# Transformer block on one core: output projection from packed heads, row sums kept in memory, three open VectorE units, layernorm pieces in the fast queue

## The chip, the cores and the metric

The kernel runs on one core of a Trainium2 chip. The time is the device time of one execution, in microseconds; the median of the runs counts. The engines that matter here are TensorE (PE, matrix products; its weight loads are PEld), VectorE (DVE), ScalarE (ACT, which makes the exponentials), GpSimd (POOL) and SyncE (SP), whose instruction queue issues every DMA of this kernel. Each engine works off its instructions strictly in order.

## What is computed

A transformer block over 2048 rows of width 640, with 32 heads of 20 columns, in bf16:

```python
x = A_x
h  = x + attention(layernorm(x)) @ wo        # qkv = layernorm(x) @ wqkv; softmax(q k^T / sqrt(20)) v, 32 heads
h2 = h + ((layernorm(h) @ w_gate) * (layernorm(h) @ w_up)) @ w_down   # 640 -> 1728 -> 640
```

The softmax needs 32 x 2048 x 2048 exponentials, and that is what the kernel is built around.

## The kernel before

**Layout.** Heads are held in 8 groups of 4. A group fills 128 partitions: each head has a slot of 32, of which 20 hold values and one holds the head's sum of exponentials; the rest is padding. `qa`/`qb` and `kT` are queries and keys per group, `vx` the values with a column of ones. `On[g]` is the normalised attention output of group g for the current block of 512 query rows, still in slots of 32, and `wo[g]` the 80 rows of the output weight that belong to it, spread over the same slots with zeros between.

**Tiles.** Scores are made in tiles `sc` of 128 partitions x 1536 columns of PSUM, two buffers, 683 tiles in all. A segment is one group in one pass: pass "0" is query block 0, passes "1", "2", "3" are whole later blocks, and "E"/"F", "C"/"D", "A"/"B" are the halves of blocks 1, 2 and 3. For each tile PE makes the scores (`emit_S`, L557), ACT takes the exponential of the tile (L573, into `E` or `El`), and PE multiplies the result with `vx` into `acc` (`emit_AV`, L795).

**VectorE's units.** Where the planner finds VectorE free, the last 512 of the 1536 columns go to it instead (`x_takes`, `emit_x`): four operations, first `xv` from the scores (L610), two on `xt` (L620, L621) and last `xe` (L615). ACT's instruction then has 1024 columns. A unit is open from its first operation to its last; at most two may be open (`len(x_open) < 2`), and `xv` and `xt` have two buffers each.

**The planner.** The order of all instructions is written out when the program is built. For each tile a planner adds up estimated costs for PE, ACT and VectorE (the dictionary `at`) and fills the time that PE has over with pieces of other work: projections, the output projection `out`, the gated layer `glu`, and `y`. For VectorE, `spare` puts pieces between: first those of the queue `hot`, then units if their segment ends soon, then the queue `aux`, then units. Where PE would run too little full-width work it inserts products whose result is not used (`keep_warm`, L508, and in `emit_S`, L553).

**Normalising a group.** When a segment is done, `acc` is copied to `asb` (L807). `norm` stores the four rows of sums to a small memory tensor (L666), loads them back spread over partitions into a column range of `sums_all` (L667), takes reciprocals (L677), stores and broadcasts them (L679, L682), and multiplies into `On[g]` (L685). Each is a DMA in SP's queue. The last group of a half (`FAST`, and the last of all) does the same on PE instead (`sums_on_pe`, `rows_to_cols`), and copies its sums to `sums_all` (L711). At the end `flag_ok` checks the range of all 512 columns of `sums_all`.

**The second half of the block.** When the groups of half a block are normalised, `add_tail` queues `out`, `glu` and `y` for it. `out_mm` multiplies 8 groups into one bank of 320 columns (L1052), adds the input rows (L1056), and the second layernorm follows (`ln2_pieces`, queued on `aux`). The last half block has nothing to hide behind: `last_tail` runs after the last exponential, and there `out_most` makes 7 products per bank (L1378) before group 7 is normalised, and `out_last` the eighth (L1382).

Of the kernel before, what the change touches and what calls it, by code (L numbers as in the profile page):

```python
# [40 lines left out]
FPW = 256  # L41
G1 = 4
SPLIT_G = {"1": 4, "2": 2, "3": 1}
QA = 3 * QB
# [47 lines left out]
def kernel(  # L92
# [80 lines left out]
    def wqk_half(c, hf):  # L173
        return (wo if hf else wqk)[c][:, 0:D].rearrange("p (m x) -> p m x", m=2)

# [417 lines left out]
    def x_takes(i):  # L593
        us, n = tiles[i]
        s = us[-1][0]
        whole = segs[s][4] == "only"
        if not whole and (aux or last_tile[s] - i < X_CHUNK):
            return False
        return (n == EW and (PASS[segs[s][0]][0] < LAST_B or room()) and last_tile[s] - i >= X_LEAST and len({u[0] for u in us if not whole and u[3] >= n - BANK or whole}) == 1
                and len(x_open) < 2 and at["dve"] < at["pe"] + PE_DVE + TOL and len(x_live) < X_OUT)  # L600

    def emit_x(ps, us):
        s = us[0][0]
        w = PASS[segs[s][0]][2]
        v = xp.tile([P, BANK], F32, name="xv", bufs=2)
        u = v[:].bitcast(U16).rearrange("p (n h) -> p n h", h=2)[:, :, 0]
        t = xp.tile([P, BANK], F32, name="xt", bufs=2)
        e = xp.tile([P, BANK], I16, name="xe", bufs=X_OUT)
        dve(608, 0)
        took = nc.vector.tensor_scalar(v[:], ps, X_SCALE, X_BASE, ALU.mult, ALU.max)  # L610
        x_live.append((s, us[-1][1], us[-1][2]))
        x_left[s] = x_left.get(s, 0) + 1

        def last():
            nc.vector.scalar_tensor_tensor(e[:], t[:], X_R, v[:], ALU.mult, ALU.add)  # L615
# [3 lines left out]
        x_open.append((s, deque([  # L619
            lambda: nc.vector.scalar_tensor_tensor(t[:], u, X_P, u, ALU.add, ALU.mult),  # L620
            lambda: nc.vector.scalar_tensor_tensor(t[:], t[:], X_Q, u, ALU.add, ALU.mult),  # L621
            last])))
        x_last[0] = x_open[-1]
        return took
# [31 lines left out]
    def read_out(b):  # L656
        return all(("om", b, t) in done for t in TAILS[b])

    def norm(s, asb):
        p, g = segs[s][0:2]  # L660
        b, c0, w = PASS[p]
        n = w // 32
        r16 = sums_all[:, col["n"]:col["n"] + n]
        col["n"] += n
        sums = dram.tile([HPG, w], F32, name="sums", tag=f"sums{w}")
        nc.sync.dma_start(sums[:], asb[DH:P:SLOT, 0:w])  # L666
        nc.sync.dma_start(r16, sums[:].rearrange("j (c f) -> (j c) f", f=n))  # L667

        due = at["dve"] + SUMS_NS

        def back():
# [4 lines left out]
            dve(130)  # L676
            nc.vector.reciprocal(ri[:], r16)  # L677
            scr = dram.tile([HPG, w], F32, name="scr", tag=f"scr{w}")
# [5 lines left out]
            def times(asb, bc, p, g, c0, w):  # L684
                nc.vector.tensor_tensor(On[g][:, c0:c0 + w], asb[:, 0:w], bc[:, 0:w], ALU.mult)  # L685
# [16 lines left out]

    def sums_to_rows(ps, w):
        n = w // SLOT
        r16 = sums_all[:, col["n"]:col["n"] + n]
        col["n"] += n
# [3 lines left out]
        nc.vector.tensor_copy(bc[:, 0:w].rearrange("p (j e) -> p j e", e=SLOT), ri[:].rearrange("p (j e) -> p j e", e=1).to_broadcast([P, n, SLOT]))  # L710
        nc.vector.tensor_copy(r16, ps[:, 0:n])  # L711
        return bc
# [6 lines left out]
    def job_norm(s, asb):  # L719
# [4 lines left out]
        dve(700, 0)  # L724
        bc = sums_to_rows(ps, w)
        yield NEXT
# [258 lines left out]
    def load_wo():  # L985
        for g in range(NG):
            nc.vector.memset(wo[g][:], 0.0)
# [5 lines left out]
            while at["pe"] < due and not now["forced"]:  # L993
                yield WAIT

    def make_identf():
# [50 lines left out]
    def out_mm(on, st, t):  # L1047
        for hf in range(2):
            ps = bank()
            cs = slice(hf * HALF, (hf + 1) * HALF)  # L1050
            for g in range(NG):
                nc.tensor.matmul(ps[:, 0:HALF], lhsT=on[g][:, t * P:(t + 1) * P], rhs=wo[g][:, cs],  # L1052
                                 start=(g == 0), stop=(g == NG - 1))
                if g == NG - 1:
                    dve(408, 136)
# [80 lines left out]
    def job_out(on, st, ts, key):  # L1136
# [229 lines left out]
    def last_tail():  # L1366
# [6 lines left out]
        def out_most(t, hf):  # L1373
            ps = ps_h[t, hf] = bank()
            cs = slice(hf * HALF, (hf + 1) * HALF)
            nc.tensor.matmul(ps[:, 0:HALF], lhsT=ident[:], rhs=st["xr"][t][:, cs], start=True, stop=False)
            for g in range(NG - 1):
                nc.tensor.matmul(ps[:, 0:HALF], lhsT=on[g][:, t * P:(t + 1) * P], rhs=wo[g][:, cs], start=False, stop=False)  # L1378

        def out_last(t):  # L1380
            for hf in range(2):
                nc.tensor.matmul(ps_h[t, hf][:, 0:HALF], lhsT=on[NG - 1][:, t * P:(t + 1) * P],  # L1382
                                 rhs=wo[NG - 1][:, hf * HALF:(hf + 1) * HALF], start=False, stop=True)
# [47 lines left out]
    def fill():  # L1431
        while step() is not None:
            pass

    def flag_ok():
        n = col["n"]
        bits = sums_all[:, 0:n].bitcast(I32)
        nc.vector.tensor_reduce(ext[:, 0:1], bits, axis=AX.X, op=ALU.min)
# [76 lines left out]
    def general():  # L1515
        st = new_st(None)
        st["res"] = {}
        with tc.For_i(0, S, P) as r0:
# [3 lines left out]
            for g in range(NG):  # L1522
# [41 lines left out]
                nc.tensor.transpose(ps[:], oq[:].rearrange("p j e -> p (j e)"), ident[:])  # L1564
                nc.vector.tensor_copy(On[g][:, 0:P], ps[:])
            for fn in (job_out(On, st, [0], None), job_glu(st, [0]), job_y(st, [0])):
# [35 lines left out]
```

## Time and profile before

| | us |
|---|---|
| median of 3 runs | 896.84 (896.48 to 897.79) |
| the profiled execution, device time | 900.67 |
| its span, first to last instruction | 898.8 |
| first exponential starts | 16.22 |
| last exponential ends (857.62 + 1.14) | 858.76 |

The profiled execution is 3.83 us above the median of the runs. The span has three parts: 16 us before the first exponential, 842.5 us in which ACT works off the 683 tiles, and 40 us after them. In the views, "idle before" is the time an engine stood still just ahead of an instruction, and the name behind the arrow is what released it. "PEclk" is the clock that TensorE was granted, as a share of full speed.

### The profile page before, as it was taken

How to read it: one execution, taken by the hardware profiler on the slowest of the kernel's cores; microseconds unless marked ns; L12 is line 12 of the kernel's file. 1: busy time of each engine (PE TensorE's matmuls, PEld its weight loads, DVE VectorE, ACT ScalarE, POOL GpSimd, SP SyncE). 2: the span in 40 equal slices, each digit the busy share in tenths (PEclk: the TensorE clock that was granted, in tenths of full speed). 3: DMA queues.
4: the chain of work that ended last, by engine and by line, in shares of the span. 5: the costliest groups of instructions: out<-in, count | busy, mean ns of one | idle time of the engine just before them, and what ended most of it. 6: DMA issues, size and time to landing. Idle time of an engine off the chain costs nothing.

```text
span 898.8 us, 21965 instructions
## 1 busy us (share of the span) xinstructions
PE 813.7 (91%) x8921; PEld 374.1 (42%) x8921; DVE 773.7 (86%) x1448; ACT 852.7 (95%) x719; POOL 31.4 (3%) x122
## 2 busy tenths in 40 slices
PE   7889999989999899889999998998899999999997
PEld 5333232222233344544444554443434455444465
DVE  7778899999999899789999998999889988889842
ACT  6999999999999999989999999999999999999951
POOL 4100000000002000001000000001000000000000
PEclk9999999999999999989999999999989999999999
DMA  6030010011034556432214334111441312010310
GB/s 198 25 65 2 1 28 25 15 36 28 14 84 112 122 146 198 112 88 66 54 51 122 81 96 107 47 30 29 121 121 45 85 31 74 15 44 9 94 38 18
DMA packets 110763, 60.15 MB, mean 67 GB/s; under 512 B 37976, under 2 KB 107652, under 8 KB 110656
## 3 DMA queue, kind: packets, MB, share of 16 engines
q1 hardware_dynamic: 110656, 58.68, 25.0%
q8 instruction: 72, 1.18, 0.6%
q14 instruction: 35, 0.29, 0.1%
HBM read 48.09 MB, written 7.28 MB: 62 GB/s over the span
## 4 chain that ended last, share of the span: by engine, by line
ACT 56%; PE 21%; issue 13%; DVE 9%; DMA 1%; SPq 0%; ACTq 0%; DVEq 0%
ACT E L573 46%; ACT El L573 10%; PE sc L557 5%; PE mi L1221 3%; PE acc L795 3%; PE f L1203 2%; PE mi L306 1%; PE mi L1052 1%; DVE xv L610 1%; PE mi L1270 1%; PE f L1270 1%; DVE xt L620 1%; DVE xt L621 1%; DVE xe L615 1%; DVE hh L1229 1%
## 5 line engine op out<-in xcount | busy, mean ns | idle before, releaser
L573 ACT ACTIVATE E<-sc 128x1536 bf16<-128x1536 f32 (+1 forms) x560 | 694.0, 1387 | 7.3 <-PE sc L557 6.0
L557 PE MATMUL sc<-qa,kT 32*128 32x256 bf16 (+1 forms) x2176 | 204.1, 320 | 23.8 <-ACT E L573 13.5
L557 PEld LDWEIGHTS <-kT 32*128 32x128 bf16 x3136 | 85.2, 92 | 223.9 <-issue 193.4
L610 DVE TENSOR_SCALAR xv<-sc 128x512 f32<-128x512 f32 x199 | 137.1, 690 | 47.3 <-PE sc L557 44.4
L573 ACT ACTIVATE El<-sc 128x1536 bf16<-128x1536 f32 (+1 forms) x123 | 159.7, 1371 | 0.6 <-PE sc L557 0.5
L795 PE MATMUL acc<-E,vx 128*32 128x256 bf16 (+1 forms) x2245 | 158.2, 315 | 0.6 <-DVE vx L271 0.6
L615 DVE SCALAR_TENSOR_TENSOR xe<-xt,xv 128x512 int16<-128x512 f32 x199 | 134.3, 681 | 0.8
L621 DVE SCALAR_TENSOR_TENSOR xt<-xt,xv 128x512 f32<-128x512 f32 x199 | 133.2, 680 | 0.6
L620 DVE SCALAR_TENSOR_TENSOR xt<-xv 128x512 f32<-128x512 uint16 x199 | 132.1, 679 | 0.3 <-DVE ri L677 0.2
L306 PE MATMUL mi<-lnT,wp 128*128 128x512 bf16 x305 | 86.5, 381 | 7.1 <-DVE qa L313 3.4
L795 PEld LDWEIGHTS <-vx 128*32 128x32 bf16 x3136 | 62.2, 96 | 62.5 <-issue 60.6
L557 PE MATMUL sc<-qb,kT 32*128 32x256 bf16 (+1 forms) x960 | 69.0, 283 | 3.4 <-ACT E L573 2.2
L1270 PE MATMUL mi<-wd,hh 128*128 128x320 bf16 x378 | 65.5, 301 | 1.1 <-DVE xr L1274 1.0
L1221 PE MATMUL mi<-ln2T,wg 128*128 128x256 bf16 x390 | 56.7, 274 | 8.6 <-DVE u L1226 7.2
L1221 PE MATMUL mi<-ln2T,wu 128*128 128x256 bf16 x390 | 55.5, 274 | 7.4 <-DVE hh L1229 7.2
L795 PE MATMUL acc<-El,vx 128*32 128x256 bf16 (+1 forms) x579 | 60.6, 294 | 0.5 <-ACT El L573 0.5
L795 PE MATMUL acc<-xe,vx 128*32 128x256 bf16 (+1 forms) x312 | 57.3, 306 | 0.0
L1270 PEld LDWEIGHTS <-hh 128*128 128x128 bf16 x448 | 37.9, 97 | 29.5 <-issue 18.2
L1221 PEld LDWEIGHTS <-wg 128*128 128x128 bf16 x390 | 33.6, 97 | 30.0 <-issue 25.3
L306 PEld LDWEIGHTS <-wp 128*128 128x128 bf16 x310 | 24.8, 97 | 50.6 <-issue 38.5
L1221 PEld LDWEIGHTS <-wu 128*128 128x128 bf16 x390 | 33.8, 97 | 28.3 <-issue 25.1
L1052 PE MATMUL mi<-wo,on 128*128 128x320 bf16 x224 | 41.6, 312 | 2.3 <-DVE xr L1056 2.2
(152 smaller groups left out, 623.0 us busy)
## 6 DMA issues: line engine op xcount, KB each, us to landing
wu<-in_B_w_up_dram SPq DMA_DIRECT2D x38, 320.0 KB
wg<-in_B_w_gate_dram SPq DMA_DIRECT2D x37, 320.0 KB
bc<-scr SPq DMA_DIRECT2D x60, 64.0 KB
bc<-scr SPq DMA_DIRECT2D x108, 32.0 KB
qsp<-qa SPq DMA_DIRECT2D x8, 384.0 KB
xr<-in_A_x_dram SPq DMA_DIRECT2D x16, 160.0 KB
out_dram<-xr SPq DMA_DIRECT2D x14, 160.0 KB
wd<-in_B_w_down_dram SPq DMA_DIRECT2D x13, 160.0 KB
```

What stands on the lines that cost most here:

```text
L306: nc.tensor.matmul(ps[:], lhsT=wslice(m, g, c), rhs=lnT[:, c, ch * QB:(ch + 1) * QB], start=(c == 0), stop=(c == KT - 1))
L557: nc.tensor.matmul(sc[:, o:o + w], lhsT=kT[g][SLOT * j:SLOT * (j + 1), kt * P:(kt + 1) * P], rhs=q_of(g, b, c0, w)[SLOT * j:SLOT * (j + 1) ...
L573: exps = nc.scalar.activation(e[:, 0:n_act], sc[:, 0:n_act], ACT.Exp, bias=EXP_BIAS, scale=SM_SCALE)
L610: took = nc.vector.tensor_scalar(v[:], ps, X_SCALE, X_BASE, ALU.mult, ALU.max)
L615: nc.vector.scalar_tensor_tensor(e[:], t[:], X_R, v[:], ALU.mult, ALU.add)
L620: lambda: nc.vector.scalar_tensor_tensor(t[:], u, X_P, u, ALU.add, ALU.mult),
L621: lambda: nc.vector.scalar_tensor_tensor(t[:], t[:], X_Q, u, ALU.add, ALU.mult),
L795: nc.tensor.matmul(acc["t"][SLOT * j:SLOT * (j + 1), 0:w], lhsT=vx[kt][:, VS * h:VS * h + SLOT], rhs=e, start=(acc["n"][j] == 0), stop=(ac ...
L1052: nc.tensor.matmul(ps[:, 0:HALF], lhsT=on[g][:, t * P:(t + 1) * P], rhs=wo[g][:, cs], start=(g == 0), stop=(g == NG - 1))
L1203: nc.tensor.matmul(ps[:, 0:n], lhsT=st["w", fp][k][:, c, f_cols(fp, f2)], rhs=st["ln2T"][:, c, c0:c0 + n], start=(c == 0), stop=(c == KT - 1))
L1221: nc.tensor.matmul(ps[:, f2 * n:(f2 + 1) * n], lhsT=st["w", fp][k][:, c, f_cols(fp, f2)], rhs=st["ln2T"][:, c, c0:c0 + n], start=(c == 0), ...
L1270: nc.tensor.matmul(ps[:, 0:HALF], lhsT=st["hh"][f // 2][:, f % 2, t * P % HW:t * P % HW + P], rhs=late["Wd"][f][:, cs], start=(f == 0), st ...
```

## The change

1. **Packed projection.** Groups 0 to 5 no longer go to `wo` and `On` in slots of 32. Their 24 heads are 480 dense rows in four pairs of tiles, `d0` to `d3`, of 128, 128, 128 and 96 rows. The multiplication of a group writes a scratch tile `on` (two buffers), and `pack` copies its heads by DMAs in SP's queue, four, or five where a head crosses a tile's end. Groups 6 and 7 stay as they were. A bank takes 6 products for 8; `out_most` 5 for 7.
2. **Sums in memory.** `sums_all` is a memory tensor of 512 columns for 128 rows. `keep_sums` stores each segment's sums there, also those of the groups normalised on PE, whose copy on VectorE goes. `read_sums` loads all of them in `last_tail`, for `flag_ok`.
3. **A third open unit.** `x_open` may hold three; `xv` gets a third buffer; `xt` keeps two, taken at the unit's second operation.
4. **Queue.** `ln2_pieces` and the multiplication `times` go to `hot`. The planner's costs for `out` are lower.

```diff
+PADDED = (6, 7)
+DENSE = ("d0", "d1", "d2", "d3")
+OUT_ROWS = {"d3": 96}
+X_OPEN = 3
-PE_NS = {"out": 6000, "glu": 23000, "y": 7000}
+PE_NS = {"out": 4900, "glu": 23000, "y": 7000}
-ALONE_NS = {"out": 4350, "glu": 15260, "y": 5710}
+ALONE_NS = {"out": 3264, "glu": 15260, "y": 5710}
-    wo = [const.tile([P, D], BF16, name=f"wo{g}") for g in range(NG)]
+    wo = {k: const.tile([P, D], BF16, name=f"wo{k}") for k in DENSE + PADDED}
-    sums_all = const.tile([P, N_SUMS], F32, name="sums_all")
+    sums_all = dram.tile([P * N_SUMS], F32, name="sums", bufs=1)
-    On = [onp.tile([P, QB], BF16, name=f"on{g}") for g in range(NG)]
+    On = {k: onp.tile([P, QB], BF16, name=f"on{k}") for k in DENSE + PADDED}
...
-                and len(x_open) < 2 and at["dve"] < at["pe"] + PE_DVE + TOL and len(x_live) < X_OUT)
+                and len(x_open) < X_OPEN and at["dve"] < at["pe"] + PE_DVE + TOL and len(x_live) < X_OUT)
-        v = xp.tile([P, BANK], F32, name="xv", bufs=2)
+        v = xp.tile([P, BANK], F32, name="xv", bufs=X_OPEN)
...
+    def pack(o, g, cols):
+        for j in range(HPG):
+            r, d = DH * (HPG * g + j), 0
+            while d < DH:
+                n = min(DH - d, P - (r + d) % P)
+                to = (r + d) % P
+                nc.sync.dma_start(On[DENSE[(r + d) // P]][to:to + n, cols], o[SLOT * j + d:SLOT * j + d + n, cols])
+                d += n
+
+    def keep_sums(asb, w):
+        n = w // SLOT
+        sums = sums_all[P * col["n"]:P * (col["n"] + n)]
+        col["n"] += n
+        nc.sync.dma_start(sums.rearrange("(j q) -> j q", j=HPG), asb[DH:P:SLOT, 0:w])
+        return sums
...
-        sums = dram.tile([HPG, w], F32, name="sums", tag=f"sums{w}")
-        nc.sync.dma_start(sums[:], asb[DH:P:SLOT, 0:w])
-        nc.sync.dma_start(r16, sums[:].rearrange("j (c f) -> (j c) f", f=n))
+        sums = keep_sums(asb, w)
+        r16 = nrm.tile([P, n], F32, name="r16", tag=f"r{n}")
+        nc.sync.dma_start(r16[:], sums.rearrange("(q f) -> q f", f=n))
...
-                nc.vector.tensor_tensor(On[g][:, c0:c0 + w], asb[:, 0:w], bc[:, 0:w], ALU.mult)
+                cols = slice(c0, c0 + w)
+                o = On[g] if g in PADDED else onp.tile([P, QB], BF16, name="on", bufs=2)
+                nc.vector.tensor_tensor(o[:, cols], asb[:, 0:w], bc[:, 0:w], ALU.mult)
+                if g not in PADDED:
+                    pack(o, g, cols)
-                aux.append(times(asb, bc, p, g, c0, w))
+                hot.append(times(asb, bc, p, g, c0, w))
...
-        nc.vector.tensor_copy(r16, ps[:, 0:n])
...
+    def out_product(ps, key, t, cs, start, stop):
+        n = OUT_ROWS.get(key, P)
+        nc.tensor.matmul(ps[:, 0:HALF], lhsT=On[key][0:n, t * P:(t + 1) * P], rhs=wo[key][0:n, cs], start=start, stop=stop)
...
-            for g in range(NG):
-                nc.tensor.matmul(ps[:, 0:HALF], lhsT=on[g][:, t * P:(t + 1) * P], rhs=wo[g][:, cs],
-                                 start=(g == 0), stop=(g == NG - 1))
+            for key in DENSE + PADDED:
+                out_product(ps, key, t, cs, key == DENSE[0], key == PADDED[-1])
...
-            aux.append(ln2_pieces(st, pair, key))
+            (hot if key is not None else aux).append(ln2_pieces(st, pair, key))
...
-            for g in range(NG - 1):
-                nc.tensor.matmul(ps[:, 0:HALF], lhsT=on[g][:, t * P:(t + 1) * P], rhs=wo[g][:, cs], start=False, stop=False)
+            for key in (DENSE + PADDED)[:-1]:
+                out_product(ps, key, t, cs, False, False)
...
-        bc = sums_to_rows(sums_on_pe(asb, HW), HW)
+        bc = sums_to_rows(sums_on_pe(asb, HW), HW, asb)
+        read_sums()
...
+    def read_sums():
+        assert col["n"] == N_SUMS
+        final["sums"] = nrm.tile([P, N_SUMS], F32, name="bc")
+        nc.sync.dma_start(final["sums"][:], sums_all[:].rearrange("(q f) -> q f", f=N_SUMS))
```

Since the planner's rules change, the order moves on every engine. Counted over the whole order, VectorE has 208 units for 199, PE 192 products of the output projection for 256, and of the products that only keep it busy 118 at L508 for 112 and 17 at L553 for 18. The number of score tiles is the same.

VectorE while the keys and queries of later groups are still being projected (`kT`, `qa`; L618, L615, L629 and L623 are a unit's four operations in turn), in the changed kernel:

```order
L618 TENSOR_SCALAR xv<-sc 128x512 x3
L317 TENSOR_SCALAR kT_146<-mi,one_row 128x512
L836 TENSOR_TENSOR qa_121<-acc,qa_121 128x512
L615 SCALAR_TENSOR_TENSOR xt<-xv 128x512 x2
L317 TENSOR_SCALAR kT_146<-mi,one_row 128x512
L629 SCALAR_TENSOR_TENSOR xt<-xt,xv 128x512 x2
L623 SCALAR_TENSOR_TENSOR xe<-xt,xv 128x512
L317 TENSOR_SCALAR kT_146<-mi,one_row 128x512
L623 SCALAR_TENSOR_TENSOR xe<-xt,xv 128x512
L615 SCALAR_TENSOR_TENSOR xt<-xv 128x512
```

Three units are begun in a row here, and the third waits with its second operation until the two others are through; before, a third could not begin.

VectorE's last stretch ahead of the last score tile's value products; the last `asb` copy is that of the last segment. Before:

```order
L615 SCALAR_TENSOR_TENSOR xe<-xt,xv 128x512 x2
L708 RECIPROCAL ri<-mi 128x8
L710 COPY bc<-ri 128x256
L711 COPY sums_all<-mi 128x8
L685 TENSOR_TENSOR on_173<-asb,bc 128x256
L731 TENSOR_TENSOR on_174<-asb,mi 128x256
L807 COPY asb<-acc 128x256
```

and now:

```order
L733 RECIPROCAL ri<-mi 128x8
L735 COPY bc<-ri 128x256
L623 SCALAR_TENSOR_TENSOR xe<-xt,xv 128x512
L755 TENSOR_TENSOR on_170<-asb,mi 128x256
L709 TENSOR_TENSOR on<-asb,bc 128x256
L1304 TENSOR_TENSOR xr<-mi,xr 128x320
L831 COPY asb<-acc 128x256
```

Group 5's multiplication of the last half (L685, now L709) moved behind group 6's (L731, now L755), and the copy of sums is gone.

SP's queue at the same place, from the last normalisation by DMA to the weights of the last part. Before:

```order
L679 DMA scr<-ri 128x8
L682 DMA bc<-scr 32x256 x4
L1280 DMA out_dram<-xr 128x640 x2
L1169 DMA E<-in_B_w_up_dram 128x5x256
L1169 DMA E<-in_B_w_gate_dram 128x5x256
```

and now:

```order
L680 DMA sums<-asb 4x256
L1310 DMA out_dram<-xr 128x640
L673 DMA ond_169<-on 20x256 x4
L680 DMA sums<-asb 4x256
L1468 DMA bc<-sums 128x512
L1310 DMA out_dram<-xr 128x640
L1199 DMA E<-in_B_w_up_dram 128x5x256
L1199 DMA E<-in_B_w_gate_dram 128x5x256
```

Four copies of heads into `d3`, two stores of sums and the load of all sums stand in the queue where two stores of output rows stood.

More of the change, by code (lines that the diff above doesn't have):

```diff
@@ L604, in emit_x, with second @@
         w = PASS[segs[s][0]][2]
-        v = xp.tile([P, BANK], F32, name="xv", bufs=2)
+        v = xp.tile([P, BANK], F32, name="xv", bufs=X_OPEN)
         u = v[:].bitcast(U16).rearrange("p (n h) -> p n h", h=2)[:, :, 0]
-        t = xp.tile([P, BANK], F32, name="xt", bufs=2)
+        t = []
+        def second():
+            t.append(xp.tile([P, BANK], F32, name="xt", bufs=2))
+            nc.vector.scalar_tensor_tensor(t[0][:], u, X_P, u, ALU.add, ALU.mult)
         e = xp.tile([P, BANK], I16, name="xe", bufs=X_OUT)
@@ L619, in emit_x @@
         x_open.append((s, deque([
-            lambda: nc.vector.scalar_tensor_tensor(t[:], u, X_P, u, ALU.add, ALU.mult),
-            lambda: nc.vector.scalar_tensor_tensor(t[:], t[:], X_Q, u, ALU.add, ALU.mult),
+            second,
+            lambda: nc.vector.scalar_tensor_tensor(t[0][:], t[0][:], X_Q, u, ALU.add, ALU.mult),
             last])))
@@ L701, in sums_on_pe, with sums_to_rows @@
         return ps
-    def sums_to_rows(ps, w):
+    def sums_to_rows(ps, w, asb):
         n = w // SLOT
-        r16 = sums_all[:, col["n"]:col["n"] + n]
-        col["n"] += n
+        keep_sums(asb, w)
         ri = nrm.tile([P, n], F32, name="ri", tag=f"ri{n}")
@@ L724, in job_norm @@
         dve(700, 0)
-        bc = sums_to_rows(ps, w)
+        bc = sums_to_rows(ps, w, asb)
         yield NEXT
@@ L1564, in general @@
                 nc.tensor.transpose(ps[:], oq[:].rearrange("p j e -> p (j e)"), ident[:])
-                nc.vector.tensor_copy(On[g][:, 0:P], ps[:])
+                o_t = On[g] if g in PADDED else onp.tile([P, QB], BF16, name="on", bufs=2)
+                nc.vector.tensor_copy(o_t[:, 0:P], ps[:])
+                if g not in PADDED:
+                    pack(o_t, g, slice(0, P))
             for fn in (job_out(On, st, [0], None), job_glu(st, [0]), job_y(st, [0])):
```

21 lines of the change are left out of this document (10 added, 11 removed).

## The prediction, made before the changed kernel ran

> **What bounds the kernel now.** I read the page first: busy shares, the slices, the chain.
>
> ```profile
> PE 813.7 (91%) x8921; PEld 374.1 (42%) x8921; DVE 773.7 (86%) x1448; ACT 852.7 (95%) x719; POOL 31.4 (3%) x122
> ACT  6999999999999999989999999999999999999951
> PEclk9999999999999999989999999999989999999999
> ACT 56%; PE 21%; issue 13%; DVE 9%; DMA 1%; SPq 0%; ACTq 0%; DVEq 0%
> ```
>
> ACT is the busiest engine and is full in all slices but the first and the last two. That is an average, so next the windows, cut at the first and the last exponential, and ACT's waits.
>
> ```profile
> 16.20:858.80 842.60, 768.72 (x8520) 338.33 (x8521) 745.19 (x1362) 835.28 (x684) 24.57 (x61) 0.99 0.25 65
> 858.80:898.80 40.00, 33.46 (x277) 26.10 (x276) 16.06 (x48) 9.91 (x24) 0.00 (x0) 0.96 0.11 32
> ACT E L573 <- PE sc L557: 6.0, 8, 2.0
> ACT El L573 <- PE sc L557: 0.5, 2, 0.3
> ```
>
> In the 842.6 us of the loop (columns: length, then PE, PEld, DVE, ACT, POOL busy) ACT works 835.28 and waits for scores 6.5, in ten places. So in the loop time is what ACT is given to do, plus those few waits; an edit on PE or VectorE is worth nothing there by itself. In the 40 us after it ACT has 9.91 us of work and PE sets the pace. The change is to be priced in these two parts separately.
>
> **Term 1, exponentials moved to VectorE: -3.8 us.** The order has 208 units for 199, so nine more tiles go through ACT with 1024 columns instead of 1536.
>
> ```profile
> L573 ACT ACTIVATE E<-sc 128x1536 bf16<-128x1536 f32 x397 | 561.3, 1511 | 4.5 <-PE sc L557 3.4 <-PE acc L795 0.4 <-ACT El L573 0.3
> L573 ACT ACTIVATE E<-sc 128x1024 bf16<-128x1024 f32 x163 | 171.7, 1082 | 2.8 <-PE sc L557 2.6 <-ACT E L573 0.2
> L573 ACT ACTIVATE El<-sc 128x1536 bf16<-128x1536 f32 x86 | 124.9, 1498 | 0.3 <-PE sc L557 0.3
> L573 ACT ACTIVATE El<-sc 128x1024 bf16<-128x1024 f32 x37 | 39.7, 1075 | 0.3 <-PE sc L557 0.2
> ```
>
> A unit saves ACT 1511 - 1082 = 429 ns, or 1498 - 1075 = 423 in the other buffer: 9 x 0.427 = 3.8 us. The third open unit therefore buys only nine, although 484 tiles went without a unit before. The reason is VectorE:
>
> ```profile
> L610 DVE TENSOR_SCALAR xv<-sc 128x512 f32<-128x512 f32 x199 | 137.1, 690 | 47.3 <-PE sc L557 44.4
> 837.23 0.69 DVE L610 TENSOR_SCALAR xv<-sc 128x512 f32<-128x512 f32 x1
> 837.84 0.41 DVE L807 COPY asb<-acc 128x256 f32<-128x256 f32 x1
> ```
>
> One operation lasts 0.69 us and the next starts 0.61 after it, so a unit is four times 0.61, 2.4 us of VectorE, and nine are 22. VectorE stands idle 842.6 - 745.2 = 97 us in the loop, 47 of them ahead of a unit's first operation, while it waits for scores. The nine fit into that, so I cost them at nothing. If they did not, see rival B.
>
> **Term 2, the tail: -1.0 us.** The chain after the last exponential:
>
> ```profile
> 859.20 0.24 PE f L1376
> 859.45 0.95 PE f L1378 x7
> 860.40 0.34 PE f L700 x4
> 860.74 0.16 PE f L1376
> 860.89 0.95 PE f L1378 x7
> 861.84 0.44 PE acc L716 x4
> 862.29 0.14 PE f L1376
> 862.42 0.95 PE f L1378 x7
> 863.37 0.27 PE f L1382 x2
> 863.65 0.14 PE f L1376
> 863.78 0.95 PE f L1378 x7
> ```
>
> Seven products take 0.95 us, 0.136 each. Each of the four banks loses two, so PE is through 8 x 0.136 = 1.09 us earlier. VectorE must keep up:
>
> ```profile
> 859.24 0.42 DVE L807 COPY asb<-acc 128x256 f32<-128x256 f32 x1 [5.98 <-PE acc L795]
> 861.07 0.29 DVE L710 COPY bc<-ri 128x256 f32<-128x256 f32 x1
> 864.91 0.89 DVE L209 BATCH_NORM_STATS2 st<-f 128x6 f32<-128x320 f32 x2 [0.22 <-PE f L1382]
> ```
>
> The sums on PE (L700) started at 860.40 and can now start 0.27 earlier, at 860.13; `asb` is there at 859.66. `bc` ends at 861.36, moves with them to 861.09, and PE asks for it at 860.74 - 0.27 + 0.16 + 0.68 = 861.31. Before the statistics of the second row tile VectorE had waited 0.22 us. The first row tile comes six products, 0.82 us, earlier, the second eight, 1.09: of the 0.27 between them 0.22 are covered and 0.05 lost. 1.0 us remains; the bounds are 1.1 and, if VectorE were late everywhere, 0.
>
> **Term 3, products taken from the loop: 0, between -4.5 and +4.6.** The loop's 28 banks lose 56 products of 0.136, 7.6 us of PE. PE is not what ACT waits for, except here:
>
> ```profile
> 285.00:295.00 10.00, 7.96 (x55) 1.64 (x53) 8.95 (x22) 9.40 (x8) 4.58 (x7) 0.83 0.52 103
> 397.00:406.00 9.00, 9.00 (x98) 4.12 (x95) 6.05 (x13) 6.68 (x6) 0.00 (x0) 0.62 0.01 2
> 651.00:664.00 13.00, 12.12 (x78) 4.26 (x79) 9.85 (x21) 11.37 (x10) 0.00 (x0) 0.74 0.84 223
> 401.40 2.05 PE L1052 MATMUL mi<-wo,on 128*128 128x320 bf16 x7
> 404.12 4.63 ACT L573 ACTIVATE E<-sc 128x1024 bf16<-128x1024 f32 x4 [2.05 <-PE sc L557]
> ```
>
> In three stretches the granted clock (third number from the right) is 0.83, 0.62 and 0.74. In the second, seven products of the projection took 2.05 us in place of 0.95, the next scores came late, and ACT stood still for 2.05 us. By ACT's busy time it was idle 0.60, 2.32 and 1.63 us in the three, 4.5 of its 6.5. A shorter bank would make such a stall shorter. But with 7.6 us less full-width work the clock could drop more often; the six more products at L508, 512 columns each and so about 0.22, return only 1.3. Both signs are open. The ends are: no such stretch left, -4.5; two more like the worst, 2 x 2.3 = +4.6. I take 0, as the three that are there are the nearest row.
>
> **Term 4, units that end later: +0.5 us.** With three open, a segment's last `xe` can stand one unit later, and the products that close the segment read it.
>
> ```profile
> L795 PE MATMUL acc<-xe,vx 128*32 128x256 bf16 (+1 forms) x312 | 57.3, 306 | 0.0
> ```
>
> Today PE never waits ahead of these products. Lower end 0; upper end, at some three of the 61 segments one operation of 0.68 each, +2.0. The row says it lies near the lower end: 0.5.
>
> **Term 5, packing and sums by DMA: 0, up to +0.5.** In the loop 158 copies of heads are added, 20 loads of `wo` go, and there are seven more stores of sums and one load.
>
> ```profile
> 845.96 1.72 SPq L682 DMA_DIRECT2D bc<-scr  x4
> SPq L667 <- DMA sums<-asb: 47.9, 38, 2.3
> 851.89 0.41 DVE L685 TENSOR_TENSOR on<-asb,bc 128x256 bf16<-128x256 f32 x1
> 852.84 0.42 DVE L731 TENSOR_TENSOR on<-asb,mi 128x256 bf16<-128x256 f32 x1 [0.54 <-PE mi L716]
> ```
>
> Four issues take SP 1.72 us, 0.43 each, so 158 are 68 us of a queue that no one computes on, in eight half blocks. Behind a pack stand the next group's reciprocals' store and weight loads; a tile lasts 842.6 / 683 = 1.23 us and a group of half a block 10.7 tiles, 13 us, five issues 2.2, so they are covered. What counts is the projection, which now waits for a landing. For all halves but the last, two more groups, 26 us, are computed after the last packed one. For the last half there is this: group 5's multiplication now stands behind group 6's, so it ends near 852.84 + 0.42 + 0.42 = 853.7. Four issues bring it to 855.4, a landing as in the second row (47.9 / 38 = 1.3, longest 2.3) to 856.7 or 857.7. PE reads it with the fourth product of the tail, after 859.4. The cover is 1.7 to 2.7 us; if it is gone, the tail waits by what is missing. The load of all sums needs two landings after 859.7, some 4 us, and VectorE reads it only here:
>
> ```profile
> 874.69 0.68 DVE L1438 TENSOR_REDUCE ext<-sums_all 128x1 f32<-128x512 int32 x1
> ```
>
> The layernorm pieces in the fast queue change what VectorE does first, not how much; the memsets and copies of sums that go add to VectorE's idle time: 0.
>
> **Sum.** -3.8 - 1.0 + 0 + 0.5 + 0 = -4.3 us. The profiled span goes from 898.8 to 894.5 and its device time from 900.67 to 896.4. The median of the runs stands 3.83 us lower than the profiled execution; taken off it, 896.84 - 4.3 = **892.5**.
>
> **The rivals.**
>
> A. *The clock gives it back.* Two more cold stretches as in term 3: -4.3 + 4.6 = +0.3, 897.1. For it: in PE's new order, ahead of the projection of block 3's first half, three score tiles in a row stand without any full-width product, and the projection follows, as at 401.40. Against it: the planner puts a pair of L508 into each of the eleven tiles before them, and the projection that follows is itself shorter. The Trainium skill, "TensorE: Matmul & The Clock Gate", section "What's actually happening", says that the clock halves after an idle window of about 3.4 us and comes back after as long a busy one; by that rule three tiles without such work are near one window, and this rival is the outcome. The half clock agrees with the 0.62 above, taken over 9 us; what counts as idle for the gate no row here shows.
>
> B. *VectorE becomes the bound: slower.* A unit's first operation also frees the score tile. With VectorE at (745.2 + 22) / 838 = 92% of the loop, a unit that starts late holds the tile, PE's scores after next are late, and ACT waits. It outweighs all gains from 6.1 / 208 = 30 ns per unit: then 898.6 and above; at 40 ns per unit 892.5 + 8.3 = 900.8. For it: first operations are already begun as soon as scores are there. Against it: VectorE waits 44.4 us for scores before them, 0.22 per unit, so it is ahead, not behind.
>
> C. *The relief counts.* The shorter banks let the cold stretches vanish: -4.3 - 4.5 = -8.8, 888.0. For it: the longest wait of ACT was behind seven products. Against it: the cold clock came before that bank did.
>
> **How the numbers follow.** Forecast 0.60, A 0.17, B 0.13, C 0.10. The forecast's own range is 890.5 to 894.6 (term 4 and 5 at their ends, one stall more or less). To leave out no more than 2 in 10 it reaches over A and half of C: **888.5 to 898.0**. A difference of 0.2%, 1.8 us, is what can be told from none. Faster: the forecast and C, less the forecast's upper edge, 0.69. Same: A and that edge, 0.17. Slower: B, and A's upper side, 0.14.
>
> **What would show it.** Term 1: 208 units, ACT's 1024-column instructions at 209, ACT busy 3.8 us less in the loop. Term 2: the tail from the last exponential to the end 39.0 us long for 40.0, five L1378 pieces of 0.68. Term 3: ACT's waits for scores near 6.5 and three or so stretches below 0.9. Term 4: a wait of PE for `xe`. Term 5: no wait of PE for a copy into `d0` to `d3`. Wrong: ACT's waits over 11 us, a wait of VectorE for a DMA ahead of a multiplication into `on`, or first operations of units that start late after their scores.

## The result, and the profile after

| | before | changed kernel |
|---|---|---|
| median, us | 896.66 (894.95 to 898.69, 6 runs) | 945.09 (942.19 to 948.6, 6 runs) |
| ratio to before | | 1.054 [1.0509, 1.0571] |
| span of the profiled execution, us | 898.8 | 944.7 |

The changed kernel is 5.4% slower, 48 us, where 0.5% faster was forecast. The page of its profile, busy engines and granted clock and the chain of waits:

```profile
PE 826.9 (88%) x8806; PEld 374.7 (40%) x8862; DVE 788.4 (83%) x1471; ACT 854.1 (90%) x719; POOL 31.1 (3%) x122
ACT  6999997998999999998998999999999999998931
PEclk9999997999999999999999999999999999999989
ACT 33%; PE 31%; DVE 16%; issue 11%; DMA 5%; SPq 2%; DVEq 0%; ACTq 0%
```

ACT has as much to do as before, but is no longer full, and its share of the chain fell from 56% to 33%: DMAs and SP's queue, 1% together before, now hold 7% of it. The same cuts as in the prediction, first exponential to last and from there to the end (length, then PE, PEld, DVE, ACT, POOL busy, clock, DMA share, GB/s):

```profile
15.75:897.81 882.06, 779.27 (x8415) 337.37 (x8469) 760.35 (x1386) 836.88 (x683) 23.98 (x60) 0.98 0.25 65
897.81:944.70 46.89, 35.31 (x268) 26.90 (x268) 16.04 (x47) 9.95 (x24) 0.00 (x0) 0.90 0.13 37
```

The loop is 39.5 us longer, the tail 6.9. In the loop ACT works 1.6 us more and stands idle 45.2 us instead of 7.3. The waits (us in all, times, longest) say for what:

```profile
ACT E L577 <- PE acc L819: 18.6, 14, 2.8
ACT E L577 <- PE sc L561: 16.6, 21, 3.4
ACT El L577 <- PE acc L819: 5.1, 4, 2.4
ACT El L577 <- PE sc L561: 4.2, 7, 1.6
DVE on L709 <- DMA bc<-scr: 16.6, 9, 4.9
PE acc L819 <- DVE asb L831: 10.4, 16, 1.1
```

Waits for scores, 6.5 us before, are 20.8. A wait that hardly was there, for the value products (L819) to give back a buffer of exponentials, went from 0.4 to 23.7. And VectorE stands 16.6 us ahead of multiplications into `on`, until a broadcast lands; before it was 0.3.

**The first kind of wait, as it happens.** The timeline of the changed kernel (start, duration; in brackets the idle time before it and what ended it), SP's queue first, then the other engines:

```profile
138.10 7.37 SPq L673 DMA_DIRECT2D ond<-on  x9
145.57 0.42 SPq L701 DMA_DIRECT2D scr<-ri  x1
147.08 1.70 SPq L704 DMA_DIRECT2D bc<-scr  x4
...
139.14 0.24 DVE L699 RECIPROCAL ri<-r 128x16 f32<-128x16 f32 x1
...
147.85 3.72 ACT L577 ACTIVATE E<-sc 128x1536 bf16<-128x1536 f32 x3
...
150.51 0.69 DVE L709 TENSOR_TENSOR on<-qa,bc 128x512 bf16<-128x512 f32 x1 [3.16 <-DMA bc<-scr]
...
152.92 0.74 DVE L317 TENSOR_SCALAR qa<-mi,shift_row 128x512 bf16<-128x512 f32 x1
...
153.71 0.58 PE L310 MATMUL mi<-lnT,wp 128*128 128x512 bf16 x1 [3.40 <-DVE qa L317]
...
154.95 1.45 ACT L577 ACTIVATE E<-sc 128x1536 bf16<-128x1536 f32 x1 [3.38 <-PE sc L561]
```

Nine copies of heads hold SP for 7.37 us. The reciprocals of the next group are ready at 139.38 (139.14 + 0.24), but their store stands behind the copies and is issued only at 145.57, and the broadcast behind the store. VectorE reaches the multiplication and stands 3.16 us, and everything behind it with it: among that the copy at L317 that empties a PSUM bank. PE stands 3.40 us for this bank, the next scores stand behind PE's instruction, and ACT stands 3.38 us. The delay is passed on undiminished through three engines that each work in order. Afterwards the clock is low (the same columns as above; before, both windows had 1.00):

```profile
150.00:155.00 5.00, 1.60 (x11) 0.33 (x6) 4.49 (x8) 1.62 (x3) 0.00 (x0) 0.82 0.10 25
155.00:160.00 5.00, 4.70 (x21) 0.91 (x20) 3.62 (x6) 3.69 (x3) 0.00 (x0) 0.50 0.03 8
```

PE was busy 1.6 of 5 us, then runs 5 us at half clock, and ACT, which works 5.3 us in these 10 us (the sum of the fifth column's figures, that of ACT), worked 9.6 before. The Trainium skill, "TensorE: Matmul & The Clock Gate", section "What's actually happening", has the clock halve after about 3.4 us of idleness and return after as much work. The 3.40 us wait and the 0.50 behind it agree with the first half of that; the return came later here, as PE was busy 4.70 us between 155 and 160 and the clock stayed at 0.50.

**The second kind**, in the same kernel's timeline at the end of a segment:

```profile
221.22 0.39 PE L819 MATMUL acc<-xe,vx 128*32 128x512 bf16 x1
...
221.92 0.68 DVE L831 COPY asb<-acc 128x512 f32<-128x512 f32 x1
222.52 0.68 DVE L623 SCALAR_TENSOR_TENSOR xe<-xt,xv 128x512 int16<-128x512 f32 x1
222.65 0.62 PE L819 MATMUL acc<-E,vx 128*32 128x512 bf16 x8 [1.04 <-DVE asb L831]
...
223.14 2.37 ACT L577 ACTIVATE E<-sc 128x1024 bf16<-128x1024 f32 x2 [2.29 <-PE acc L819]
```

The segment's last `xe` product comes at 221.22. Only then can `acc` be copied out, and only after that copy may the next segment's value products begin. All exponentials of the tiles since then are still held; there are six buffers of them, eight late in the kernel, and when they are used up ACT stops, here for 2.29 us. PE's wait is 1.04 us, ACT's twice that: what ACT loses is the whole time that the segment stayed open, less what the buffers hold. That is read from this one place; the experiment with one more buffer, below, tests it.

### The profile page after: what moved, and what is told of

Read it like the earlier page. It is cut to its first block, busy times and chain, and to the rows that moved or that the text cites. A ratio compares the mean times of both kernels' runs of the same rounds, so it can differ in the third digit from the quotient of the medians.

```text
span 944.7 us, 22021 instructions
## 1 busy us (share of the span) xinstructions
PE 826.9 (88%) x8806; PEld 374.7 (40%) x8862; DVE 788.4 (83%) x1471; ACT 854.1 (90%) x719; POOL 31.1 (3%) x122
## 4 chain that ended last, share of the span: by engine, by line
ACT 33%; PE 31%; DVE 16%; issue 11%; DMA 5%; SPq 2%; DVEq 0%; ACTq 0%
ACT E L577 26%; PE sc L561 8%; ACT El L577 6%; PE mi L1251 6%; PE acc L819 6%; DVE xv L618 3%; PE mi L1300 3%; DMA scr<-ri 2%; PE mi L310 2%; DVE xt L615 2%; DVE xt L629 2%; PE f L1233 2%; DVE xe L623 2%; DMA bc<-scr 1%; SPq L704 1%
## 5 line engine op out<-in xcount | busy, mean ns | idle before, releaser
L618 DVE TENSOR_SCALAR xv<-sc 128x512 f32<-128x512 f32 x208 | 143.1, 688 | 51.1 <-PE sc L561 48.2
L819 PE MATMUL acc<-E,vx 128*32 128x256 bf16 (+1 forms) x2252 | 159.0, 320 | 10.9 <-DVE asb L831 8.3
L577 ACT ACTIVATE El<-sc 128x1536 bf16<-128x1536 f32 (+1 forms) x120 | 153.5, 1337 | 9.7 <-PE acc L819 5.1
L623 DVE SCALAR_TENSOR_TENSOR xe<-xt,xv 128x512 int16<-128x512 f32 x208 | 140.5, 679 | 0.3
L629 DVE SCALAR_TENSOR_TENSOR xt<-xt,xv 128x512 f32<-128x512 f32 x208 | 139.6, 680 | 0.2
L615 DVE SCALAR_TENSOR_TENSOR xt<-xv 128x512 f32<-128x512 uint16 x208 | 139.0, 681 | 0.0
L819 PEld LDWEIGHTS <-vx 128*32 128x32 bf16 x3136 | 67.3, 97 | 83.9 <-issue 81.3
L1251 PE MATMUL mi<-ln2T,wg 128*128 128x256 bf16 x410 | 60.3, 275 | 10.4 <-DVE u L1256 8.4
L819 PE MATMUL acc<-xe,vx 128*32 128x256 bf16 (+1 forms) x326 | 66.2, 310 | 0.3 <-issue 0.3
L1251 PE MATMUL mi<-ln2T,wu 128*128 128x256 bf16 x410 | 60.1, 275 | 4.5 <-DVE hh L1259 3.9
L819 PE MATMUL acc<-El,vx 128*32 128x256 bf16 (+1 forms) x558 | 61.1, 297 | 2.1 <-DVE asb L831 2.1
L310 PEld LDWEIGHTS <-wp 128*128 128x128 bf16 x310 | 24.4, 97 | 53.1 <-issue 42.6
L1256 DVE CAST u<-mi 128x512 bf16<-128x512 f32 x49 | 33.5, 684 | 8.7 <-PE mi L1251 8.3
```

What stands on the lines that cost most here:

```text
L310: nc.tensor.matmul(ps[:], lhsT=wslice(m, g, c), rhs=lnT[:, c, ch * QB:(ch + 1) * QB], start=(c == 0), stop=(c == KT - 1))
L577: exps = nc.scalar.activation(e[:, 0:n_act], sc[:, 0:n_act], ACT.Exp, bias=EXP_BIAS, scale=SM_SCALE)
L615: nc.vector.scalar_tensor_tensor(t[0][:], u, X_P, u, ALU.add, ALU.mult)
L623: nc.vector.scalar_tensor_tensor(e[:], t[0][:], X_R, v[:], ALU.mult, ALU.add)
L629: lambda: nc.vector.scalar_tensor_tensor(t[0][:], t[0][:], X_Q, u, ALU.add, ALU.mult),
L819: nc.tensor.matmul(acc["t"][SLOT * j:SLOT * (j + 1), 0:w], lhsT=vx[kt][:, VS * h:VS * h + SLOT], rhs=e, start=(acc["n"][j] == 0), stop=(ac ...
```

## The experiments

In the expectations P is the theory that the copies of heads cost the time, X that the third open unit does, H that the fast queue does. The runs were taken at different times, each beside runs of the kernel before, so the ratio is what compares them: "over before" is (ratio - 1) x 896.7 us. The intervals reach some 1.5 to 4 us to each side.

| kernel | what differs from the changed kernel | median, us | ratio [95%] | over before, us |
|---|---|---|---|---|
| changed | | 945.09 | 1.054 [1.0509, 1.0571] | 48.4 |
| open2 | two open units | 922.35 | 1.0268 [1.0233, 1.0302] | 24.0 |
| nopack | no packing | 912.74 | 1.0173 [1.0148, 1.0198] | 15.5 |
| nopack_open2 | neither | 897.41 | 1.0016 [0.9997, 1.0034] | 1.4 |
| pack_on_pool | copies issued by GpSimd | 922.27 | 1.0295 [1.0252, 1.0337] | 26.5 |
| pool_open2 | same, two open units | 906.2 | 1.0119 [1.0099, 1.0139] | 10.7 |
| copies_unread_sp | nopack_open2 and 158 copies nobody reads, SP | 916.19 | 1.0218 [1.019, 1.0246] | 19.5 |
| copies_unread_sp_half | same, 65 copies | 904.35 | 1.0088 [1.0058, 1.0118] | 7.9 |
| copies_unread_pool | same, 158 copies, GpSimd | 900.06 | 1.0041 [1.0025, 1.0057] | 3.7 |
| packed_order_no_copies | two open units, PE's shorter banks, no copies | 905.56 | 1.009 [1.0072, 1.0108] | 8.1 |
| pack_by_memory | two open units, packed by way of memory | 918.45 | 1.025 [1.0225, 1.0274] | 22.4 |
| pack_by_memory_late | same, read back five tiles later | 909.55 | 1.0148 [1.0115, 1.0181] | 13.3 |
| nopack_far | no packing, third unit only far from a segment's end | 900.97 | 1.0066 [1.0043, 1.0089] | 5.9 |
| pool_more_buffers | as pack_on_pool, one more late buffer of exponentials | 916.35 | 1.0243 [1.0218, 1.0268] | 21.8 |

### Which part of the change costs it

```diff
-X_OPEN = 3
+X_OPEN = 2
```

> The changed kernel with two open units for three (X_OPEN = 2); packing, sums in memory and the fast queue stay. Theory P (the copies of heads hold up SP's queue, 0.71 us an issue, so broadcasts land late and VectorE waits for them): almost no change, 938 to 946 us, VectorE still waits some 16 us for broadcasts and the tail is still 47 us. Theory X (with three open units a segment's last operation comes late, the accumulator is freed late and the buffers of exponentials run out): ACT's 23.7 us of waits for buffers (released by the value products) fall to a few, 915 to 923 us. Theory H (the layernorm pieces and multiplications in the fast queue push evacuations back): no change, 940 to 950 us.

```diff
-PADDED = (6, 7)
-DENSE = ("d0", "d1", "d2", "d3")
+PADDED = (0, 1, 2, 3, 4, 5, 6, 7)
+DENSE = ()
...
-PE_NS = {"out": 4900, "glu": 23000, "y": 7000}
+PE_NS = {"out": 6000, "glu": 23000, "y": 7000}
...
-ALONE_NS = {"out": 3264, "glu": 15260, "y": 5710}
+ALONE_NS = {"out": 4350, "glu": 15260, "y": 5710}
...
-                out_product(ps, key, t, cs, key == DENSE[0], key == PADDED[-1])
+                out_product(ps, key, t, cs, key == PADDED[0], key == PADDED[-1])
```

> The changed kernel without the packing: all eight groups stay in slots of 32, eight products to a bank; three open units, sums in memory and the fast queue stay. Theory P: VectorE's waits for broadcasts go to about 0 and the tail to 40 us; 16.6 + 8 us and more come back, 893 to 915 us. Theory X: only the tail's 8 us come back, 925 to 938 us, ACT's waits for buffers stay above 15 us. Theory H: 930 to 940 us.

Both edits together:

> Without the packing and with two open units; what is left of the change is the sums in memory and the fast queue. Theories P and X together: as before, 894 to 900 us. Theory H: still 910 us or more, with VectorE's evacuations late.

Without both the time is that of before, 1.0016 [0.9997, 1.0034]: the sums in memory and the fast queue cost nothing that can be told, and theory H is out. open2 came out in theory X's range and nopack in theory P's, so each of the two theories explains a part and neither the whole. From there the third unit alone adds 14.1 us, the packing alone 22.6, and both 47.0, 10.3 more than the sum. In nopack ACT's waits are mostly of the second kind:

```profile
ACT E L577 <- PE acc L819: 8.6, 10, 2.3
ACT E L577 <- PE sc L561: 5.2, 7, 1.3
```

In the same view of open2 they are of the first, and VectorE waits for loads of sums:

```profile
ACT E L577 <- PE sc L561: 19.5, 20, 3.7
DVE ri L699 <- DMA r<-sums: 10.2, 3, 4.4
```

So they are two costs, not one. What was expected of VectorE's waits for broadcasts held only in part: they are 3.3 us in open2, where theory P had some 16, and 4.7 in nopack, where it had about 0. (The third unit also buys less than the 208 units suggest: without packing there are 202 units with three open and 198 with two.)

### SP's queue, or the copies themselves

```diff
-                nc.sync.dma_start(On[DENSE[(r + d) // P]][to:to + n, cols], ...)
+                nc.gpsimd.dma_start(On[DENSE[(r + d) // P]][to:to + n, cols], ...)
```

> The changed kernel with the copies of heads issued from GpSimd's queue instead of SP's; nothing else differs. Theory P: what SP does no longer waits behind copies, so VectorE's waits for broadcasts fall from 16.6 to below 4 us and the tail comes down by some us, 905 to 925 us. Theory X: VectorE's waits shrink too but ACT's waits for buffers stay near 20 us, 925 to 938 us. If the copies are late by themselves and not the queue: PE waits for them, no better than 940 us.

> The changed kernel with the copies issued from GpSimd's queue and with two open units. If the whole cost of packing was SP's queue and the whole rest the third unit: 894 to 898 us, the tail 0.6 us shorter than before. If the copies cost something besides the queue (a wait of PE for a landing, traffic): 900 to 908 us.

The same copies in GpSimd's queue, which has little else to do: 21.9 us less with three open units, 13.3 less with two. In pack_on_pool ACT's waits for scores fall from 20.8 to 6.3 us and VectorE's for broadcasts from 16.6 to 6.5, while ACT's waits for value products stay at 23.8: only the first kind goes with SP's queue. But pool_open2 stays 9.3 us above nopack_open2, so the queue is not all of the packing's cost. The next three leave everything as in nopack_open2, PE's order too, and add the copies alone, into tiles that nothing reads:

```diff
+    spare_t = [onp.tile([P, QB], BF16, name=f"cp{k}") for k in range(3)]
...
-                nc.sync.dma_start(On[DENSE[(r + d) // P]][to:to + n, cols], ...)
+                nc.sync.dma_start(spare_t[(r + d) // P % 3][to:to + n, cols], ...)
...
-                if g not in PADDED:
+                if g < 6:
                     pack(o, g, cols)
```

> No packing and two open units, PE's order as in that run (897.4 us), but the 158 copies of heads are issued from SP's queue all the same, into tiles that nobody reads. Theory P (the queue's time alone): 915 to 923 us, as with packing and two units (922.4), with VectorE waiting for loads of sums or broadcasts. If the cost comes from PE waiting for packed rows or from the new order of PE: 896 to 902 us.

With `g < 3`, which leaves 65 of the 158 copies:

> The same with the copies of groups 0 to 2 only, about half of them. If the cost is in proportion to SP's time: 906 to 910 us. If it sets in only where a queue's slack is used up: 897 to 904 us.

With `nc.gpsimd`:

> The same with all 158 copies issued from GpSimd's queue, unread. Packing from GpSimd's queue with two units took 906.2 us, 9 more than no packing. If these 9 are the copies' traffic or their issue on GpSimd: 904 to 908 us. If they are PE's new order with shorter banks or its waits for packed rows: 896 to 899 us.

158 copies that no engine waits for cost 18.1 us in SP's queue and 2.3 in GpSimd's, hardly more than the noise; 65 cost 6.5, about 0.1 us for each in both doses. (The half dose, 904.35, fell between the two ranges expected, and so did 900.06 in GpSimd's queue.) It is the place in the queue that costs, not the bytes and not a reader. How long one issue takes, from the views of a line's instructions (minimum, median, maximum in ns), for the changed kernel's copies and broadcasts:

```profile
L673 SPq DMA_DIRECT2D ond<-on x158: 554/713/1399, 138.1 to 899.9; - x158
L704 SPq DMA_DIRECT2D bc<-scr x168: 311/414/1646, 124.7 to 891.3; - x168
```

and for copies_unread_sp, where the line is 674:

```profile
L674 SPq DMA_DIRECT2D cp<-on x158: 554/713/1316, 135.5 to 870.4; - x158
```

and for copies_unread_pool, on GpSimd:

```profile
L674 POOL DMA_DIRECT2D cp<-on x158: 502/510/755, 133.0 to 853.3; - x158
```

158 x 0.713 is 113 us of SP, in lumps of up to nine. What stood behind them in copies_unread_sp is in its waits: weights, broadcasts and sums. The last row is what ACT then waits for, 3.3 us in nopack_open2:

```profile
PEld L1252 <- DMA wg<-in_B_w_gate_dram: 8.3, 7, 2.2
DVE on L710 <- DMA bc<-scr: 6.9, 5, 2.3
...
DVE ri L700 <- DMA r<-sums: 3.2, 2, 2.4
...
ACT E L578 <- PE sc L562: 16.5, 21, 2.3
```

In copies_unread_pool the wait for `bc` is 0.8 us.

### The rest of the packing: PE's shorter banks alone

```diff
-X_OPEN = 3
+X_OPEN = 2
+    for k in DENSE:
+        nc.gpsimd.memset(On[k][:], 0.0)
...
-                if g not in PADDED:
-                    pack(o, g, cols)
```

Groups 0 to 5 are left out of the output here: their dense tiles hold zeros. The order on PE is that of pool_open2.

> Six dense products to a bank and two open units, PE's order word for word that of packing from GpSimd's queue (906.2 us), but no copies are issued at all: the dense tiles hold zeros, so groups 0 to 5 are left out of the output. If PE's order with shorter banks costs the 6 us that unread copies from GpSimd's queue (900.1 us) do not explain: 902 to 906 us. If PE's reads of the copied rows or the landings cost them: 895 to 898 us, the tail's 0.6 us below no packing (897.4 us).

8.1 us over before, 6.7 over nopack_open2, with no copy at all. With it the parts add up: 1.4 + 6.7 for the order + 2.3 for copies in GpSimd's queue is 10.4, and pool_open2 has 10.7; with 18.1 for SP's queue it is 26.2, and open2 has 24.0. Where the order costs time, the timeline of packed_order_no_copies shows at its longest wait:

```profile
617.41 0.35 SPq L691 DMA_DIRECT2D r<-sums  x1
...
620.09 0.20 DVE L701 RECIPROCAL ri<-r 128x8 f32<-128x8 f32 x1 [2.50 <-DMA r<-sums]
...
621.97 0.68 DVE L1259 TENSOR_TENSOR hh<-mi,u 128x512 bf16<-128x512 f32 x1
...
622.71 1.80 PE L1251 MATMUL mi<-ln2T,wu 128*128 128x256 bf16 x10 [2.58 <-DVE hh L1259]
...
625.17 1.45 ACT L579 ACTIVATE El<-sc 128x1536 bf16<-128x1536 f32 x1 [2.82 <-PE sc L563]
```

The sums' load is issued at 617.41 and VectorE stands for it 2.50 us, then PE for `hh`, then ACT. With other costs for `out` the planner puts other work side by side, and here it put reciprocals ahead of their sums. Of this kernel's loop, 847.5 us for 840.4 in nopack_open2, this one place is 2.8. ACT's others there are short, at most 1.5 us, and nearly all for scores, some in or just behind stretches of low clock (0.72 at 600 to 605, 0.77 at 795 to 800); which share is the clock's and which the order's was not separated.

### Packing with fewer issues

Each group is stored whole to memory and its rows read back densely, all by SP, with two open units:

```diff
+        nc.sync.dma_start(tmp[:], o[:, cols])
...
+                nc.sync.dma_start(On[DENSE[r // P]][r % P:r % P + DH * whole, cols], rows_[0:whole, 0:DH, :])
...
+        later(2, back)
```

> Two open units; the packing stays in SP's queue but each group is stored whole to memory and read back as dense rows two tiles later: 2 to 4 issues per group for 4 or 5, and those from memory should take SP 0.35 to 0.43 us as its others do, not 0.71. Theory P (it is SP's time per issue): about half of the 25.7 us or more comes back, 900 to 910 us. If it is the dependence chain through SP and not the issue time: 915 us or more.

918.45 is far from the first range and hardly better than open2. The waits in its SP queue show why:

```profile
SPq L678 <- DMA pk<-on: 38.8, 25, 4.9
```

The reading back stands at the head of the queue until the store has landed, 38.8 us in all: of what was saved in issues, a large part was paid in standing. A queue is as much taken by a wait as by an issue. With `later(5, back)`:

> Packing by way of memory with two open units (918.5 us), but the dense rows are read back five tiles after the store instead of two, so that SP does not stand waiting for the store's landing (38.8 us there). SP's time for packing falls from some 94 us to 55. Theory P: the cost falls in proportion, 907 to 912 us. If SP's time is not what counts: 917 us or more.

That row falls to 12.3 us, and the time to 909.55, 9.1 us less over before.

### The third unit

```diff
-                and len(x_open) < X_OPEN and ...
+                and len(x_open) < (X_OPEN if last_tile[s] - i >= 8 else 2) and ...
```

This on top of nopack:

> Without packing; a third unit may open only where its segment has at least 8 tiles left (order: 199 units, for 202 with a third unit anywhere and 198 with two). Theory X, that only a third unit near a segment's end costs: 895 to 900 us, ACT's waits for buffers from 10.7 to below 3 us. If a third open unit costs wherever it stands (VectorE too full): 905 to 913 us.

ACT's waits for value products fall from 10.7 to 0.7 us, and the time over before from 15.5 to 5.9: two thirds of the third unit's cost lie where a segment ends. With them goes most of the use, as 199 units are left of 202. What remains, 4.5 us over nopack_open2, goes with VectorE's waits for `bc`, 5.6 us here and 0.5 there; that these cause it was not tried. With so few third units left, the run says little of what one far from a segment's end would cost. The expected time was missed by 1 us.

```diff
-E_BUFS, E_LATE = 6, 2
+E_BUFS, E_LATE = 6, 3
```

The planner still counts eight buffers, so that the order is that of pack_on_pool.

> Packing from GpSimd's queue, three open units, the instruction order unchanged, but three late buffers of exponentials in place of two (nine in all from tile 204 on, six before). Theory X: ACT's waits for buffers, 23.8 us, lose a good part of what lies behind tile 204 (each is 1.3 to 2.8 us long and one buffer more covers one tile, 1.2 us): 8 to 14 us less, 908 to 916 us. If those waits only show that PE is late for other reasons: 919 us or more, the waits renamed to scores.

One more buffer in the late part of the kernel halves the waits for value products, 23.8 to 11.9. It does so only where it was added: before the first late buffer is used, at about 277 us, they were 6.2 and are 6.1; after that they were 17.6 and are 5.8. So the buffers are what runs out. Not all of it comes back as time, since ACT's waits for scores rise from 6.3 to 9.5 us: over before it is 4.7 us less, hardly more than the noise of the two runs, where 8 to 14 were expected. More buffers in the early part were not tried.

## Why the prediction was wrong

**What bounds the kernel** was right and was then not applied: loop time is ACT's work plus its waits. Every term was priced by an engine's work; the change acted on waits. Term 5 failed as a step, terms 3 and 4 in their size: 18.1 + 8.6, 6.7 and 14.1 us, as worked out below, are 47.5 of the 48.4. Terms 1 and 2 brought less than priced.

**Term 1** was right in what it counted:

```profile
L577 ACT ACTIVATE E<-sc 128x1024 bf16<-128x1024 f32 x169 | 175.3, 1061 | 20.5 <-PE acc L819 16.0 <-PE sc L561 4.0 <-ACT E L577 0.2
L577 ACT ACTIVATE El<-sc 128x1024 bf16<-128x1024 f32 x40 | 41.7, 1048 | 4.6 <-PE acc L819 2.4 <-PE sc L561 2.1
```

169 and 40 are the 209 instructions forecast. But ACT's busy time rose 1.6 us where 3.8 were to go. The missing 5.4 us are in the trace as well. An exponential of 1536 columns lasts 1.45 to 1.49 us, but where nothing is in the way the next one starts 1.34 us after it (mean of 430 cases), so that the two overlap. Ahead of a stall nothing overlaps, and ACT shows about 0.13 us more work at each. Summed over all 46 waits and the shorter gaps this is 7.7 us, against 2.2 in the kernel before: 5.5 more. ACT's added work is therefore a consequence of its waits.

**Term 2** had the mechanism and not its cover. Where no copy is late the shorter banks bring 0.4 us (tail 39.54 in packed_order_no_copies, 39.94 in nopack_open2) for the 1.0 forecast. The banks themselves are shorter by the 1.08 us that were priced; 0.20 are lost again because 13 value products stand behind the last exponential instead of 6, 0.18 in the four products that spread group 7's reciprocals (0.62 us for 0.44), and 0.3 at the very end. In the changed kernel the tail is 46.9, because of term 5:

```profile
892.78 3.54 SPq L673 DMA_DIRECT2D ond<-on  x5
894.22 0.42 DVE L709 TENSOR_TENSOR on<-asb,bc 128x256 bf16<-128x256 f32 x1 [4.88 <-DMA bc<-scr]
...
897.51 3.06 SPq L673 DMA_DIRECT2D ond<-on  x4
...
901.72 0.45 PE L1025 MATMUL f<-wod,ond 96*128 96x320 bf16 x1 [2.82 <-DMA ond<-on]
...
903.16 1.27 PE L1025 MATMUL f<-wod,ond 128*128 128x320 bf16 x4
```

The multiplication ends at 894.64, but its four copies leave only at 897.51, behind five others and two stores. PE stands 2.82 us, and the banks after it run at half clock, four products in 1.27 us instead of 0.54. The 4.88 us that VectorE stands ahead of the multiplication are not the copies' doing: with the copies in GpSimd's queue (pack_on_pool) they are still there, but the copies leave soon after and the tail is 40.2 us long:

```profile
877.01 0.43 DVE L709 TENSOR_TENSOR on<-asb,bc 128x256 bf16<-128x256 f32 x1 [4.93 <-DMA bc<-scr]
877.73 2.04 POOL L673 DMA_DIRECT2D ond<-on  x4 [7.50 <-DVE on L709]
```

**Term 3**, 0 with both signs open, was +6.7 us (packed_order_no_copies over nopack_open2), above its upper end of +4.6. Rival A had the sign. It looked for the cost in the clock alone; a part of it is a reciprocal that the new order put ahead of its sums.

**Term 4**, 0.5 us with 2.0 at most, was 14.1, or 15.8 with the copies in GpSimd's queue. The mechanism was named: units end later, and the products that close a segment read them. The price counted PE's own wait for a unit's last operation, 0.68. That wait never came (0.3 us ahead of these products in the changed kernel, and none of it for VectorE); PE stands one step later, 10.4 us ahead of the next segment's products, until `acc` is copied out. The price left out that `acc` is one accumulator and the exponentials have six buffers, so that a late close stops the value products of the next segment and then ACT.

**Term 5** failed as a step. It priced an issue at 0.43 us from the row of `bc` (measured 0.71), but above all it called SP "a queue that no one computes on" and asked only whether the packed tiles are read in time. In the loop PE never waited for them, and VectorE once, 0.5 us, for its scratch tile. What waited stood behind the copies: `scr`, `bc`, sums and weights. That is 18.1 us, and with three open units 8.6 more, as the third unit costs 24.4 us beside SP's copies and 15.8 beside GpSimd's; what the tail lost, 46.9 us for 40.2, is among these. The Trainium skill, "DMA: Bandwidth & Descriptors", section "Issuing engines are not separate DMA queues", says that issuing from several engines only saves the time on the sequencer, which is usually small beside the DMA itself. Here that time was worth 13.3 and 21.9 us, because other transfers on which an in-order engine waits stood behind it.

**Rival B** foresaw that VectorE comes late and that PE and then ACT wait for it, but its reason does not hold. VectorE is not the bound: it still waits 48.2 us for scores ahead of first operations (44.4 before). It is held up by DMAs, and in the place shown what it is late with is not a first operation but the emptying of a PSUM bank. **Rival C** is refuted: the loop has nine stretches at half clock for three, 0.98 for 0.99 on average. Of the signs that were to show the prediction wrong two came true (the third, first operations that start late after their scores, was not measured): ACT's waits over 11 us, and a wait of VectorE for a DMA ahead of a multiplication into `on`.

## What to carry to other kernels

A queue that computes nothing can still be on the path: for every DMA added, list what stands behind it in the same queue and which in-order engine waits for that, and put copies that nobody waits for soon into another queue. Where a change lets work end later, follow it to what it keeps occupied (an accumulator, buffers), and count how many tiles these last; the wait of the engine that ends late is the smallest part. A kernel whose order is planned from costs of engines alone has its slack at landings and buffers unrecorded, and a new order, even a shorter one, can spend it unseen.

## What was not expected of the hardware

Issue time depends on what is issued, and where: a copy of up to 20 rows from one SBUF tile to another took SP 0.713 us, a broadcast of 32 rows from memory 0.414, and the same copy took GpSimd 0.510. And a single stall of about 3.4 us was followed by 5 us at a granted clock of 0.50, so that ACT worked 5.3 us in 10 where it had worked 9.6.
